# A fused attention and feed-forward kernel: which PSUM tiles are divided, one group of scores moved, the last unit's q and k turned by DMA, and the tail's attention outputs in a row

## The chip, the cores and the metric

The kernel runs on one core of one Trainium2 chip. The metric is device time in microseconds (us); a time is the median of several runs. Profiles are of one execution each.

## The reference

Inputs are q, k and v (8 batches, 12 heads, 448 rows, 64 columns, float32), w_in (768 x 2048) and w_out (2048 x 768).

```python
scores = scale * np.matmul(q, k.transpose(0, 1, 3, 2))        # scale = 1/8
m = np.max(scores, axis=-1, keepdims=True)
e = np.exp(scores - m)
attn = e / (np.sum(e, axis=-1, keepdims=True) + np.exp(-m) + 1e-09)
attn_out = np.matmul(attn, v)
x = attn_out.transpose(0, 2, 1, 3).reshape(B * S, H * D)      # 3584 x 768
h = x @ w_in
sp = np.where(h > 20.0, h, np.log1p(np.exp(np.minimum(h, 20.0))))
g = h * np.tanh(sp)                                           # Mish
out = g @ w_out                                               # 3584 x 768
```

## The kernel before

**Tiling.** Heads are taken in pairs, 48 of them, six to a batch. Each q or k of a pair is loaded as [112, 2, 256] float32 (row r of a head is 4p + t, so a partition holds four rows), cast to bf16 on GpSimd (POOL), and turned on TensorE (PE): four transposes of [112, 128] each for q and k go to a PSUM bank (`transpose_pair`), and `evac_qk` copies them to SBUF as qT and kT [128, 448], q on VectorE (DVE) with the scale 1/8, k on ScalarE (ACT). From pair 12 on POOL also copies the last 64 rows of one head and the first 64 of the other out of qT to a small tile (`q_rests`, two copies).

The scores of a pair are four steps s: three with two 128-row matmuls, one for each head, in two PSUM banks, and one (s = 3) for the 64 rows left of each head, in one bank. For each step DVE takes the negated row maxima (negm, line 289) and ACT the exponentials with their sums (line 300) into en (bf16). `denominators` and `normalise` divide by the sum; then one DMA transpose from SyncE's queue (SP) turns the whole of en to eT (line 339), after which PE makes the attention output (`av_pair`, line 372), which DVE casts to xT (line 381). eT has three buffers.

The feed-forward part of a batch is mm1 (xT by w_in, line 395, blocks f of 128 columns of the hidden layer with Mish on ACT, line 401, giving gT) and mm2 (gT by w_out, line 461, copied to o_sb by DVE and stored from SP).

**Stages.** A head loop takes pairs 0 to 5. Then `for u in range(2, 20)` goes through units of three pairs: u = 2 to 15 with attention (pairs 3u to 3u + 2), u = 16 to 19 a tail without. A unit is twelve steps n (exponentials of step n, then what is emitted behind them), followed by eight mm1 blocks f = 0 to 7 of batch (u − 2) // 2. From u = 4 on mm2 of earlier batches is cut into fills of two matmuls and put between. In units 4 to 15 the order in a step is written out in a table, GROUPED (GROUPED_LATE_AV for u = 5): ("fill", k) is k fills, ("sc", (i, ...)) are the scores of steps i of the unit, ("av0", i) and ("av1", i) the attention output of pair i of the unit before, in the first bank of score tile 0 or 1. In u = 16 the outputs of the last three pairs stand behind steps n = 0, 6 and 9 (`LAST_AV_AT`), in an mo tile each. While mm1 of a unit runs, the three pairs are normalised: the first two by DVE (behind f = 0 and f = 3), the third by POOL (behind f = 4), and the next unit's q and k are turned on PE behind f = 1, 3 and 5. Its first three score steps are ahead of f = 7.

**PSUM.** There are eight banks. Up to u = 3 three score tiles of two banks each (sc0 to sc2) and two tiles of one bank (mo) stand in one pool. At the end of u = 3 `banks_apart` gives that pool back and takes a new one: four banks of their own (b0 to b3), one tile of two banks (bb) and two of one (m0, m1). A bank on its own is released by its own reader and not by that of its neighbour. A tile of a new pool waits until the old pool's tiles that lay there have no users left.

From then on mm1's blocks use banks by MISH_BANK: 0 is the second bank of score tile 0, 1 a free mo tile, 2 the tile m1.

**Queues.** Work is in program order on each engine. SP's queue has all loads of q, k and v (issued in steps n = 0, 3, 6 for later pairs), the DMA transposes of en, and the stores. POOL has the casts of q, k and v, the copies to q_rests, the third normalise, and the DMAs that bring w_in and w_out in pieces in units 2 to 4.

Of the kernel before, what the change touches and what calls it, by code (L numbers as in the profile page):

```python
# [19 lines left out]
def kernel(  # L20
# [32 lines left out]
    def pool(name, bufs, space=None):  # L53
# [14 lines left out]
    mid_pool = pool("mid", 1)  # L68


    psum_of = tc.tile_pool(name="ps", bufs=1, space=PS)
    psum = psum_of.__enter__()
    sc_pairs = [
        psum.tile([128, 2, 512], FP32, tag=f"sc{i}", name=f"sc{i}") for i in range(3)
    ]
    sc_banks = [[t[:, j, :] for j in range(2)] for t in sc_pairs]
    mo_tiles = [psum.tile([128, 512], FP32, tag=f"mo{i}", name=f"mo{i}") for i in range(2)]
    mo_free = deque(mo_tiles)

    def banks_apart():  # L80

        flush_late()
        assert len(mo_free) == 2
        psum_of.__exit__(None, None, None)
        ps = pool("ps2", 1, PS)
        own = [ps.tile([128, 512], FP32, tag=f"b{i}", name=f"b{i}") for i in range(4)]
        last = ps.tile([128, 2, 512], FP32, tag="bb", name="bb")
        sc_pairs[:] = [None, None, last]
        sc_banks[:] = [own[0:2], own[2:4], [last[:, j, :] for j in range(2)]]
        mo_tiles[:] = [ps.tile([128, 512], FP32, tag=f"m{i}", name=f"m{i}") for i in range(2)]  # L90
        mo_free.clear()
        mo_free.append(mo_tiles[0])

    ident = singles.tile([128, 128], BF16)
    make_identity(nc, ident)
# [11 lines left out]
    for t_ in en_bufs:  # L107
# [2 lines left out]


    GROUP_FROM = 2 * HP
    q_rests = [
        singles.tile([128, 2, 64], BF16, tag=f"qr{i}", name=f"qr{i}") for i in range(UNIT_PAIRS)
    ]
# [59 lines left out]
    def cast_pair(p, with_v=True):  # L175
        if p >= N_PAIRS:
            return
        q_f, k_f = loaded[p][:2]
        q_bf = bf_pool.tile([SP_, NT, 2, D], BF16, tag="q_bf", name="q_bf")
        k_bf = bf_pool.tile([SP_, NT, 2, D], BF16, tag="k_bf", name="k_bf")  # L180
        v_bf = bf_pool.tile([SP_, 2, NT * D], BF16, tag="v_bf", name="v_bf", bufs=9)
        by_t = "p h (t d) -> p t h d"
        cast_q, cast_k = nc.gpsimd.tensor_copy, nc.gpsimd.tensor_copy
        if p == 0:
            cast_q, cast_k = nc.vector.tensor_copy, nc.scalar.copy
        cast_q(out=q_bf, in_=q_f.rearrange(by_t, t=NT))  # L186
        cast_k(out=k_bf, in_=k_f.rearrange(by_t, t=NT))  # L187
        casted[p] = (q_bf, k_bf, v_bf)
        if with_v:
            cast_v(p)  # L190

    def transpose_pair(p, bank=None):
# [16 lines left out]
        own = [] if bank is not None else [ps, ps_k] if p == 0 else [ps]  # L209
        qkT[p] = (by_s, own)  # L210

    def evac_qk(p, act=False):
        if p >= N_PAIRS:
            return
        (q_ps, k_ps), own = qkT[p]
        mo_free.extend(own)
        qT = qk_pool.tile([128, S], BF16, tag="qT", name="qT")
        kT = qk_pool.tile([128, S], BF16, tag="kT", name="kT")
        qkT[p] = (qT, kT)
        if act:  # L220
            nc.scalar.mul(qT, q_ps[:, 0:S], SCALE)
        else:
            nc.vector.tensor_scalar(
                out=qT, in0=q_ps[:, 0:S], scalar1=SCALE, scalar2=None, op0=ALU.mult
            )
        if p >= GROUP_FROM:
            q_rest = q_rests[p % UNIT_PAIRS]
            nc.gpsimd.tensor_copy(out=q_rest[0:64, 0, :], in_=qT[0:64, 384:S])
            nc.gpsimd.tensor_copy(out=q_rest[64:128, 1, :], in_=qT[64:128, 0:64])
# [252 lines left out]
    for g in range(B // 2):  # L482
# [23 lines left out]
        [("sc", (6,))],  # L506
        [],
        [("av1", 1), ("fill", 2)],
        [("sc", (7,)), ("fill", 2), ("sc", (8, 9)), ("fill", 4)],
        [("sc", (10,))],  # L510
        [],
        [("av0", 2), ("fill", 4), ("sc", (11,)), ("fill", 4)],
# [7 lines left out]
        [("sc", (6,))],  # L520
        [],
        [("av1", 0), ("fill", 2)],
        [("sc", (7,)), ("fill", 2), ("sc", (8, 9)), ("fill", 4)],
        [("sc", (10,))],
        [],
        [("av0", 1), ("sc", (11,))],
# [2 lines left out]
        [],  # L529
    )  # L530
    LATE_AV = first_mm2 + 1
    MISH_BANK = (0, 1, 2, 0, 1, 2, 1, 2)
    to_gather = deque()

    BY_POOL = 4
    LEAD = UNIT_PAIRS + 1
    LOAD_AT = (0, 3, 6)
    LAST_AV_AT = (0, 6, 9)
    HEAD = HP

    BY_PE = (2, 4, HEAD - 1, HEAD, HEAD + 1)
# [56 lines left out]
    for u in range(UNITS_PER_B, N_UNITS + 2 * UNITS_PER_B):  # L598
# [3 lines left out]
            filler.extend(mm2_part(*part))  # L602
        total, done, acc = sum(w for _, w in filler), 0, 0.0
        p0 = u * UNIT_PAIRS
        grouped = attn and p0 >= GROUP_FROM
        if u == N_UNITS:
            mo_free.append(mo_tiles[1])
# [2 lines left out]
        for n in range(steps):  # L610
# [6 lines left out]
            if grouped:  # L617
# [23 lines left out]
                        cast_pair(at + LEAD - 1)  # L641
                if u - UNITS_PER_B < len(W_AT):
                    load_w(W_AT[u - UNITS_PER_B].get(n, 0))
                continue
            if late_tp:
                evac_qk(p0 + 2)
# [26 lines left out]

        moe = u < N_UNITS + UNITS_PER_B
        b, w = (u - UNITS_PER_B) // UNITS_PER_B, u % UNITS_PER_B
        nxt = p0 + UNIT_PAIRS
# [5 lines left out]
        for f in range(FF_U):  # L682
            if f == FF_U - 1 and to_group and nxt < N_PAIRS:
                for s in range(3):
                    scores(nxt * STEPS + s)
            if moe:
                bank = sc_banks[0][0] if f == 1 else None
                if to_group:
                    bank = (sc_banks[0][1], None, mo_tiles[1])[MISH_BANK[f]]
                mm1_mish(b, w * FF_U + f, bank)  # L690
                if f == 2 and to_gather:
                    gather_mid(to_gather.popleft())
            if u == UNITS_PER_B and f in (2, 6):
                load_w(1)
            if not attn:
                continue
            if f == 0:
                denominators(att[p0]["whole"])
                normalise(todo[0], dma=todo[0] not in BY_PE)
            if f in (1, 3, 5):  # L700
                transpose_pair(nxt + f // 2, bank=f // 2 % 2)
                evac_qk(nxt + f // 2)
                if f == 1 and u > first_mm2:
                    cast_pair(nxt + UNIT_PAIRS - 1)
            if not to_group and f in (4, 6):
                scores_ahead(nxt * STEPS + f // 2 - 1)
            if f == FF_U - 1 and not to_group:
                scores_ahead(nxt * STEPS + 3)
            if f == 3:
                normalise(todo[1], dma=todo[1] not in BY_PE)  # L710
            if f == 4:
# [40 lines left out]
```

## Time and profile before

| | |
|---|---|
| median of 3 runs | 475.01 us (475.08, 474.40, 475.01) |
| profiled execution | 474.54 us |
| its span | 472.5 us |
| mean granted TensorE clock | 0.981 of full speed |
| PE busy | 437.3 us |
| ACT busy | 345.3 us |
| DVE busy | 339.0 us |
| POOL busy | 193.6 us |

The span is from the first to the last instruction in the profile; the rest of the execution's time lies around it. Busy times are sums over an engine's instructions, with overlaps counted once; they don't say which of the engines a stretch of the program waits for.

In the profiled execution unit 4 begins at 102.3 us, unit 5 at 127.5, unit 6 at 153.4; units 6 to 14 take 25.56 us each. mm1 of unit 15 begins at 399.1 us and the tail at 408.25.

Rows of a timeline have the start, the duration, engine, line, operation, output and inputs and a count; in square brackets stands the time for which the engine was idle ahead of it and what ended that. SPq and POOLq are DMA issues on those queues.

### The profile page before, as it was taken

What the parts mean: (1) busy time and instruction counts of PE and PEld (TensorE: products, weight loads), DVE (VectorE), ACT (ScalarE), POOL (GpSimd) and SP (SyncE); (2) the same over time, 40 slices, a digit from 0 to 9 for tenths busy, and PEclk for the clock granted to TensorE, in tenths of its full rate; (3) what the DMA queues carried; (4) which work ended last, traced back from release to release, by engine and by line L of the source; (5) the groups of instructions that cost most, each with busy time, mean ns of one, the idle gap of its engine ahead of it and who ended that gap; (6) DMA issues with size and microseconds to landing.
All of it is one profiled execution on the core that took longest, in us unless ns stands there. A gap on an engine that the chain in (4) does not pass through costs nothing.

```text
span 472.5 us, 8903 instructions
## 1 busy us (share of the span) xinstructions
PE 437.3 (93%) x3048; PEld 235.9 (50%) x3048; DVE 339.0 (72%) x723; ACT 345.3 (73%) x919; POOL 193.6 (41%) x365
## 2 busy tenths in 40 slices
PE   4565887799999999999999999999999999999997
PEld 2233444454544464555555554646454555555565
DVE  4788987958777897879787888788787978320021
ACT  5979787769797888979797979798897979312300
POOL 4876808364515354443636163525444360300000
PEclk9998698899999999999999999999999999999999
DMA  8999959999999979899989989998989794960213
GB/s 222 225 238 214 246 86 238 181 168 203 207 230 265 209 199 204 246 197 266 181 210 219 239 165 248 217 224 226 201 237 216 216 185 103 168 147 1 68 33 102
DMA packets 202382, 90.37 MB, mean 191 GB/s; under 512 B 159073, under 2 KB 198881, under 8 KB 202337
## 3 DMA queue, kind: packets, MB, share of 16 engines
q1 hardware_dynamic: 194848, 83.51, 80.9%
q0 software_dynamic: 7488, 6.29, 8.8%
q8 instruction: 24, 0.39, 0.3%
q14 instruction: 22, 0.17, 0.1%
HBM read 45.61 MB, written 11.01 MB: 120 GB/s over the span
## 4 chain that ended last, share of the span: by engine, by line
PE 75%; DVE 2%; DMA 1%; ACT 1%; issue 1%; POOL 0%; SPq 0%; DVEq 0%; POOLq 0%
PE m L461 32%; PE m L395 21%; PE b L372 6%; PE b L395 6%; PE b L263 4%; PE bb L263 2%; PE b L204 1%; PE bb L204 1%; PE m L271 1%; DMA q_f<-in_q_dram 1%; DVE negm L289 1%; PE m L372 1%; DVE o_sb L448 1%; ACT en L300 0%; POOL q_bf L186 0%
## 5 line engine op out<-in xcount | busy, mean ns | idle before, releaser
L461 PE MATMUL m<-w_out_sb,gT 128*128 128x384 bf16 (+1 forms) x896 | 141.8, 304 | 0.7 <-DVE o_sb L448 0.7
L395 PE MATMUL m<-xT,w_in_sb 128*128 128x448 bf16 x552 | 115.4, 352 | 0.0
L461 PEld LDWEIGHTS <-gT 128*128 128x128 bf16 x896 | 80.6, 98 | 59.1 <-issue 20.7
L395 PEld LDWEIGHTS <-w_in_sb 128*128 128x128 bf16 x768 | 71.6, 98 | 67.5 <-issue 9.7
L401 ACT ACTIVATE gT<-m 128x448 bf16<-128x448 f32 x92 | 50.2, 547 | 68.7 <-PE m L395 68.7
L333 POOL TENSOR_SCALAR en<-en,rden 128x448 bf16<-128x448 bf16 x122 | 76.4, 645 | 52.9 <-DVE rden L325 41.2
L289 DVE TENSOR_REDUCE negm<-b 128x1 f32<-128x448 f32 x144 | 79.9, 617 | 24.3 <-PE b L266 24.3
L300 ACT ACTIVATE en<-b,negm 128x448 bf16<-128x448 f32 x144 | 89.6, 646 | 0.0
L186 POOL CAST q_bf<-q_f 112x512 bf16<-112x512 f32 x47 | 28.9, 615 | 111.9 <-DMA q_f<-in_q_dram 111.2
L448 DVE COPY o_sb<-m 128x384 f32<-128x384 f32 (+1 forms) x64 | 32.2, 503 | 48.1 <-PE m L461 44.3
L335 DVE TENSOR_SCALAR en<-en,rden 128x448 bf16<-128x448 bf16 x214 | 66.0, 377 | 0.5
L300 ACT ACTIVATE en<-sc,negm 128x448 bf16<-128x448 f32 x84 | 52.8, 647 | 8.6 <-DVE negm L289 4.6
L289 DVE TENSOR_REDUCE negm<-sc 128x2 f32<-128x896 f32 (+1 forms) x48 | 45.5, 968 | 10.9 <-PE sc L266 4.0
L300 ACT ACTIVATE en<-bb,negm 128x448 bf16<-128x448 f32 x72 | 45.2, 638 | 5.8 <-DVE negm L289 5.8
L289 DVE TENSOR_REDUCE negm<-bb 128x2 f32<-128x896 f32 x36 | 39.0, 1082 | 0.0
L395 PE MATMUL b<-xT,w_in_sb 128*128 128x448 bf16 x168 | 36.5, 352 | 2.5 <-ACT en L300 1.8
L372 PE MATMUL b<-eT,v_bf 112*64 112x448 bf16 x288 | 34.1, 357 | 0.0
L173 POOL CAST v_bf<-v_f 112x512 bf16<-112x512 f32 x48 | 29.9, 622 | 6.5 <-DMA v_f<-in_v_dram 6.2
L187 POOL CAST k_bf<-k_f 112x512 bf16<-112x512 f32 x47 | 29.2, 621 | 6.3 <-DMA k_f<-in_k_dram 5.7
L300 ACT ACTIVATION_READ_ACCUMULATOR en<-b,negm 128x1 f32 x144 | 31.5, 219 | 0.0
L372 PEld LDWEIGHTS <-v_bf 112*64 112x64 bf16 x384 | 19.5, 111 | 19.2 <-issue 12.6
L263 PE MATMUL sc<-kT,qT 64*128 64x448 bf16 x36 | 16.7, 479 | 12.6 <-ACT en L300 11.2
(75 smaller groups left out, 573.1 us busy)
## 6 DMA issues: line engine op xcount, KB each, us to landing
q_f<-in_q_dram SPq DMA_DIRECT2D x48, 224.0 KB, 4.7
k_f<-in_k_dram SPq DMA_DIRECT2D x48, 224.0 KB, 4.9
v_f<-in_v_dram SPq DMA_DIRECT2D x48, 224.0 KB, 5.2
w_in_sb<-in_moe_w_in_dram POOLq DMA_DIRECT2D x12, 256.0 KB, 6.2
w_out_sb<-in_moe_w_out_dram POOLq DMA_DIRECT2D x8, 384.0 KB, 6.6
out_dram<-o_sb SPq DMA_DIRECT2D x7, 336.0 KB, 3.3
out_dram<-o_sb SPq DMA_DIRECT2D x8, 288.0 KB, 4.0
out_dram<-o_sb SPq DMA_DIRECT2D x8, 240.0 KB, 4.1
```

The source lines that it names most:

```text
L173: nc.gpsimd.tensor_copy(out=casted[p][2], in_=loaded.pop(p)[2])
L187: cast_k(out=k_bf, in_=k_f.rearrange(by_t, t=NT))
L263: nc.tensor.matmul(sc[0][:, 0:S], lhsT=qT[0:64, qa : qa + 128], rhs=kA, start=True, stop=True)
L289: nc.vector.tensor_reduce(out=negm, in_=scored, axis=AX.X, op=ALU.max, negate=True)
L300: nc.scalar.activation(out=st["en"][:, :, c, 0:SP_], in_=sc[bk][:, 0:S].rearrange("q (j c) -> q j c", j=NT), func=AF.Exp, bias=st["negm"][ ...
L333: nc.gpsimd.tensor_scalar(scalar2=1.0, op0=ALU.mult, op1=ALU.mult, **args)
L335: nc.vector.tensor_scalar(scalar2=None, op0=ALU.mult, **args)
L372: nc.tensor.matmul(av[h * 64 : (h + 1) * 64, 0:S], lhsT=v_bf[:, h, j * D : (j + 1) * D], rhs=e_h, start=(j == 0), stop=(j == NT - 1),)
L395: nc.tensor.matmul(h_ps[:, 0:S], lhsT=w_in_sb[:, dm, ff * 128 : (ff + 1) * 128], rhs=xT[b][:, dm, :], start=(dm == 0), stop=(dm == DM_T - 1),)
L401: nc.scalar.activation(out=gT[b][:, ff, :], in_=h_ps[:, 0:S], func=AF.Mish)
L448: nc.vector.tensor_copy(out=o_sb[:, cols], in_=st["o"][:, 0:n_cols])
L461: nc.tensor.matmul(st["o"][:, 0:n_cols], lhsT=src[:, ff, c0 : c0 + 128], rhs=w_out_sb[:, ff, cols], start=(ff == 0), stop=(ff == FF_T - 1),)
```

## The change

Five edits:

- **PSUM.** sc2 and the two mo tiles now stay in a pool of their own for the whole program; only sc0 and sc1 are in a pool that `banks_apart` gives back, for four banks of their own. As in the kernel before, one mo tile is taken out of the free list there. The first mm1 after it takes its banks in another order, FIRST_MISH_BANK, which begins with the mo tiles.
- **Mish banks.** The fourth mm1 block of a unit writes the first bank of score tile 0 (new number 3) instead of the bank of the first block.
- **Score order.** In both tables the scores of steps 8 and 9 come behind one fill instead of two; the fill goes behind them.
- **Turns by DMA.** q and k of pairs 45 and 46 (two of the last unit's three) are not turned on PE. POOL casts q with the scale in it, and two DMA transposes for each pair on SP, behind steps 8 and 11 of u = 14, write qT and kT. Their copies to q_rests go behind f = 3.
- **Tail.** In u = 16 the three attention outputs come one after the other behind n = 9, in the first bank of score tile 0, 1 and 2. The last pair's normalise in u = 15 is on DVE instead of POOL.

```diff
-    psum_of = tc.tile_pool(name="ps", bufs=1, space=PS)
-    psum = psum_of.__enter__()
-    sc_pairs = [
-        psum.tile([128, 2, 512], FP32, tag=f"sc{i}", name=f"sc{i}") for i in range(3)
-    ]
-    sc_banks = [[t[:, j, :] for j in range(2)] for t in sc_pairs]
+    psum = pool("ps", 1, PS)
+    last_pair = psum.tile([128, 2, 512], FP32, tag="sc2", name="sc2")
     mo_tiles = [psum.tile([128, 512], FP32, tag=f"mo{i}", name=f"mo{i}") for i in range(2)]
     mo_free = deque(mo_tiles)
+    pairs_of = tc.tile_pool(name="ps_pairs", bufs=1, space=PS)
+    psum = pairs_of.__enter__()
+    sc_pairs = [
+        psum.tile([128, 2, 512], FP32, tag=f"sc{i}", name=f"sc{i}") for i in range(2)
+    ] + [last_pair]
+    sc_banks = [[t[:, j, :] for j in range(2)] for t in sc_pairs]
 
     def banks_apart():
         flush_late()
+        mo_tiles[:] = mo_free
         assert len(mo_free) == 2
-        psum_of.__exit__(None, None, None)
-        ps = pool("ps2", 1, PS)
+        mo_free.pop()
+        pairs_of.__exit__(None, None, None)
+        ps = pool("ps_banks", 1, PS)
         own = [ps.tile([128, 512], FP32, tag=f"b{i}", name=f"b{i}") for i in range(4)]
-        last = ps.tile([128, 2, 512], FP32, tag="bb", name="bb")
-        sc_pairs[:] = [None, None, last]
-        sc_banks[:] = [own[0:2], own[2:4], [last[:, j, :] for j in range(2)]]
-        mo_tiles[:] = [ps.tile([128, 512], FP32, tag=f"m{i}", name=f"m{i}") for i in range(2)]
-        mo_free.clear()
-        mo_free.append(mo_tiles[0])
+        sc_pairs[0:2] = [None, None]
+        sc_banks[0:2] = [own[0:2], own[2:4]]
...
+    TURN_BY_DMA = (N_PAIRS - UNIT_PAIRS, N_PAIRS - UNIT_PAIRS + 1)
...
-        cast_q(out=q_bf, in_=q_f.rearrange(by_t, t=NT))
+        if p not in TURN_BY_DMA:
+            cast_q(out=q_bf, in_=q_f.rearrange(by_t, t=NT))
+        else:
+            nc.gpsimd.tensor_scalar(
+                out=q_bf, in0=q_f.rearrange(by_t, t=NT),
+                scalar1=SCALE, scalar2=1.0, op0=ALU.mult, op1=ALU.mult,
+            )
...
+    def turn_by_dma(p):
+        pair = [qk_pool.tile([128, S], BF16, tag=t, name=t) for t in ("qT", "kT")]
+        for dst, src in zip(pair, casted[p]):
+            nc.sync.dma_start_transpose(
+                out=dst.rearrange("c (t q) -> c t q", q=SP_),
+                in_=src.rearrange("q t h d -> q (t h d)"),
+            )
+        qkT[p] = pair
+
+    def rest_of(p):
+        qT, q_rest = qkT[p][0], q_rests[p % UNIT_PAIRS]
+        nc.gpsimd.tensor_copy(out=q_rest[0:64, 0, :], in_=qT[0:64, 384:S])
+        nc.gpsimd.tensor_copy(out=q_rest[64:128, 1, :], in_=qT[64:128, 0:64])
...
-        [("sc", (7,)), ("fill", 2), ("sc", (8, 9)), ("fill", 4)],
+        [("sc", (7,)), ("fill", 1), ("sc", (8, 9)), ("fill", 5)],
...
-    MISH_BANK = (0, 1, 2, 0, 1, 2, 1, 2)
+    MISH_BANK = (0, 1, 2, 3, 1, 2, 1, 2)
+    FIRST_MISH_BANK = (1, 2, 0, 1, 2, 0, 1, 2)
...
-    LAST_AV_AT = (0, 6, 9)
+    TURN_AFTER = (8, 11)
+    LAST_AV_AT = 9
...
+                if n in TURN_AFTER and nxt + TURN_AFTER.index(n) in TURN_BY_DMA:
+                    turn_by_dma(nxt + TURN_AFTER.index(n))
...
-            elif u == N_UNITS and n in LAST_AV_AT:
-                av_pair(p0 - UNIT_PAIRS + LAST_AV_AT.index(n))
+            elif u == N_UNITS and n == LAST_AV_AT:
+                for i in range(UNIT_PAIRS):
+                    av_pair(p0 - UNIT_PAIRS + i, bank=sc_banks[i][0])
...
-                    bank = (sc_banks[0][1], None, mo_tiles[1])[MISH_BANK[f]]
+                    order = FIRST_MISH_BANK if nxt == GROUP_FROM else MISH_BANK
+                    bank = (sc_banks[0][1], None, mo_tiles[1], sc_banks[0][0])[order[f]]
...
-                transpose_pair(nxt + f // 2, bank=f // 2 % 2)
-                evac_qk(nxt + f // 2)
+                if nxt + f // 2 not in TURN_BY_DMA:
+                    transpose_pair(nxt + f // 2, bank=f // 2 % 2)
+                    evac_qk(nxt + f // 2)
...
                 normalise(todo[1], dma=todo[1] not in BY_PE)
+                for p in TURN_BY_DMA:
+                    if p // UNIT_PAIRS == u + 1:
+                        rest_of(p)
...
-                normalise(todo[2], dma=todo[2] not in BY_PE, on_pool=True)
+                normalise(todo[2], dma=todo[2] not in BY_PE, on_pool=u + 1 < N_UNITS)
```

More of the change, by code (lines that the diff above doesn't have):

```diff
@@ L226, in evac_qk @@
         if p >= GROUP_FROM:
-            q_rest = q_rests[p % UNIT_PAIRS]
-            nc.gpsimd.tensor_copy(out=q_rest[0:64, 0, :], in_=qT[0:64, 384:S])
-            nc.gpsimd.tensor_copy(out=q_rest[64:128, 1, :], in_=qT[64:128, 0:64])
+            rest_of(p)
         if p == 0 or own and not act:
@@ L522 @@
         [("av1", 0), ("fill", 2)],
-        [("sc", (7,)), ("fill", 2), ("sc", (8, 9)), ("fill", 4)],
+        [("sc", (7,)), ("fill", 1), ("sc", (8, 9)), ("fill", 5)],
         [("sc", (10,))],
@@ L604 @@
         p0 = u * UNIT_PAIRS
+        nxt = p0 + UNIT_PAIRS
         grouped = attn and p0 >= GROUP_FROM
@@ L675 @@
         b, w = (u - UNITS_PER_B) // UNITS_PER_B, u % UNITS_PER_B
-        nxt = p0 + UNIT_PAIRS
         todo = sorted(range(p0, nxt), key=lambda p: p in BY_PE)
@@ L710 @@
                 normalise(todo[1], dma=todo[1] not in BY_PE)
+                for p in TURN_BY_DMA:
+                    if p // UNIT_PAIRS == u + 1:
+                        rest_of(p)
             if f == 4:
-                normalise(todo[2], dma=todo[2] not in BY_PE, on_pool=True)
+                normalise(todo[2], dma=todo[2] not in BY_PE, on_pool=u + 1 < N_UNITS)
         if attn and u + 1 < N_UNITS:
```

## The prediction

> **What bounds the kernel now.** I read the page first: the busy times by engine, then the chain that ended last.
>
> ```profile
> PE 437.3 (93%) x3048; PEld 235.9 (50%) x3048; DVE 339.0 (72%) x723; ACT 345.3 (73%) x919; POOL 193.6 (41%) x365
> PE 75%; DVE 2%; DMA 1%; ACT 1%; issue 1%; POOL 0%; SPq 0%; DVEq 0%; POOLq 0%
> ```
>
> TensorE (PE) carries the end. An average over stages does not say where it can be shortened, so I next read the stretches of the units. One in the steady part:
>
> ```profile
> 204.59:230.15 25.56, 25.56 (x182) 13.57 (x183) 20.92 (x47) 21.53 (x57) 11.13 (x23) 1.00 1.05 216
> ```
>
> The columns are the stretch, its length, then the busy us (and instructions) of PE, weight loads, DVE, ACT and POOL, the granted clock and two DMA columns. PE is busy for all 25.56 us. In such a unit (u=6 to u=14) an edit is worth something only if it takes instructions off PE or removes a stall between them, and there is none left. So the gains must come from the places where PE stalls: the start of u=4 (the new PSUM banks), u=4 and u=5, and the tail. I looked for them in PE's timeline, where a bracket is idle time and its releaser.
>
> **A: two score tiles divided, not all PSUM tiles renewed.** The last products of u=3 and the first matmul block (mm1) after the bank change, from the timeline of all engines:
>
> ```profile
> 88.79 1.71 PE L372 MATMUL mo<-eT,v_bf 112*64 112x448 bf16 x16
> ...
> 90.48 1.15 DVE L381 CAST xT<-mo 128x448 bf16<-128x448 f32 x2
> ...
> 91.52 0.65 ACT L300 ACTIVATE en<-sc,negm 128x448 bf16<-128x448 f32 x1
> ...
> 92.31 0.92 PE L395 MATMUL b<-xT,w_in_sb 128*128 128x448 bf16 x4 [1.81 <-ACT en L300]
> ```
>
> Before, all eight banks are given back and taken anew, so the block waits for the last exponential of the old pool (91.52 + 0.65 = 92.17). After, the first block writes an mo tile, which stays, and waits only for that tile's cast: the first of two casts, 90.48 + 1.15/2 = 91.06. The gain on PE is 92.31 − 91.2 = 1.1 us. The second block takes the other mo tile (cast over at 91.63) and starts 1.14 us after the first, and the third takes a divided bank at about 93.4, past 92.17: no new wait.
>
> **B and C.** Stalls of u=4, from PE's timeline, and one steady unit's third group of scores, from the timelines of DVE and PE:
>
> ```profile
> 117.89 0.35 PE L395 MATMUL b<-xT,w_in_sb 128*128 128x448 bf16 x1 [0.29 <-DVE xT L381]
> ...
> 121.32 1.30 PE L395 MATMUL b<-xT,w_in_sb 128*128 128x448 bf16 x6 [0.41 <-ACT gT L401]
> ```
>
> ```profile
> 214.55 0.61 DVE L381 CAST xT<-b 128x448 bf16<-128x448 f32 x1
> ...
> 214.79 0.81 PE L461 MATMUL m<-w_out_sb,gT 128*128 128x384 bf16 x4
> 215.54 0.36 PE L263 MATMUL b<-kT,qT 64*128 64x448 bf16 x1
> ...
> 215.74 0.35 PE L263 MATMUL b<-kT,qT 64*128 64x448 bf16 x1
> ...
> 215.93 2.22 DVE L289 TENSOR_REDUCE negm<-b 128x1 f32<-128x448 f32 x4 [0.24 <-PE b L266]
> ```
>
> B gives the fourth Mish block a bank of its own instead of the first block's, which takes away the 0.41 us at 121.32. C moves the products sc(8, 9) ahead of one fill of two matmuls, half of the row of four: (215.54 − 214.79)/2 = 0.37 us. The DVE waits 0.24 us for these scores now and the scores would come 0.37 us sooner, so DVE and ACT run up to 0.24 us earlier in each grouped unit. PE issues the same work in another order, so in steady units it gains nothing. The second pair's bank is free when the cast at 214.55 ends (215.16); its new start, 215.74 − 0.37 = 215.37, clears that by 0.2 us. If that cover went, each of twelve units would lose what the cast is late, at most 0.37 us. In u=4 the earlier DVE takes up to 0.24 of the 0.29 us at 117.89. A, B and C together bring PE 1.1 + 0.4 + 0.25 = 1.75 us forward at the end of u=4.
>
> **What of that survives u=5.** There the transposes of the next keys wait for POOL's casts, which wait for loads on SP's queue. SP rows, the POOL rows and the DMA queues between 121.9 and 124.4 us (packets, mean us, share of the stretch), then POOL and PE in u=5:
>
> ```profile
> 95.25 4.28 SPq L339 DMA_TRANSPOSE eT<-en  x1
> ...
> 99.83 4.33 SPq L339 DMA_TRANSPOSE eT<-en  x1
> ...
> 121.86 14.86 SPq L339 DMA_TRANSPOSE eT<-en  x3
> ```
>
> ```profile
> 100.04 4.34 POOL L333 TENSOR_SCALAR en<-en,rden 128x448 bf16<-128x448 bf16 x7 [1.40 <-DVE rden L325]
> ...
> 117.89 1.48 POOL L169 DMA_DIRECT2D w_out_sb<-in_moe_w_out_dram  x2
> ...
> 147.53 0.62 POOL L187 CAST k_bf<-k_f 112x512 bf16<-112x512 f32 x1
> ```
>
> ```profile
> q0 software_dynamic: 659, 0.49, 130.5%
> ```
>
> ```profile
> 148.20 0.37 PE L204 MATMUL b<-ident,k_bf 112*128 112x112 bf16 x4 [0.26 <-POOL k_bf L187]
> ...
> 151.26 0.37 PE L204 MATMUL b<-ident,k_bf 112*128 112x112 bf16 x4 [0.22 <-POOL k_bf L187]
> ```
>
> PE reaches these two transposes 0.26 and 0.22 us too early already; whatever it arrives sooner is waited away unless the casts move. The casts hang on u=5's loads, and these stand on SP behind the three transposes issued from 121.86, which take 14.86 instead of about 13 us. In their first 2.5 us the only queue that moves data is POOL's (q0, the w_out pieces issued up to 119.37). Those pieces stand on POOL behind casts of earlier loads, behind u=3's transposes on SP. What A can close there is SP's idle time between u=3's transposes: 99.83 − 99.53 = 0.30, and from 99.83 + 4.33 = 104.16 to the end of POOL's normalise (104.38) 0.22 us, together 0.5. The first transpose's own input hangs on the exponentials of u=3 and does not move. So the chain moves by 0.45 to 0.5 us; if u=4's transposes, issued some 1.7 us sooner, also begin moving sooner, by up to 1.75. The least is 0.25 (only one gap closes). I take 0.7, near the end that rows carry.
>
> The Trainium skill ("DMA: Bandwidth & Descriptors", section "Queues, rings and completion order") says that each DMA engine takes turns between the queues for which it has work, packet by packet. By that the transposes would have begun at 121.86 beside the w_out pieces, and would begin sooner when issued sooner; the trace does not agree so far, since the one row of that stretch is q0's. By the rule the sum would be that of the first rival.
>
> **D: q and k of pairs 45 and 46 turned by DMA.** PE and SP in u=14 and at the start of u=15, and the tile eT between 375 and 400 us (issue ns least, median, most; then us to landing):
>
> ```profile
> 381.18 0.36 PE L204 MATMUL bb<-ident,q_bf 112*128 112x112 bf16 x4
> ...
> 381.57 1.30 PE L395 MATMUL m<-xT,w_in_sb 128*128 128x448 bf16 x6
> ...
> 387.55 0.95 PE L372 MATMUL b<-eT,v_bf 112*64 112x448 bf16 x8
> ```
>
> ```profile
> 371.26 0.46 SPq L143 DMA_DIRECT2D v_f<-in_v_dram  x1
> 377.94 13.34 SPq L339 DMA_TRANSPOSE eT<-en  x3
> ```
>
> ```profile
> 374.21 0.62 POOL L187 CAST k_bf<-k_f 112x512 bf16<-112x512 f32 x1 [0.18 <-DMA k_f<-in_k_dram]
> ```
>
> ```profile
> L339 SPq DMA_TRANSPOSE eT<-en x3: 4207/4327/4591, 377.9 to 387.0; - x3
> DMA to landing us min/median/max: 6.1/7.1/7.8
> ```
>
> Eight transposes of a pair take PE from 381.18 to 381.57, 0.39 us. Two pairs: 0.8 us off PE in a stage where PE never idles. Two evacuations on DVE and two on ACT go with them, which bring nothing there. What is added: four DMA transposes on SP and two scaled casts on POOL. SP is idle from 371.72 to 377.94. An attention transpose has 28 blocks of 128 columns and issues in 4.33 us, one of q or k has 4, so by blocks 0.62 us each and 2.5 us in all; the upper bound is 4.33 us each. Pair 46's key cast ends at 374.83, so its two turns would end by about 376.1, before 377.94. I take the block price because a load issues in 0.46 us (371.26): no more than that can be fixed, and with 0.46 fixed and 4/28 of the rest a turn costs 1.0, still over by 377. The scaled cast takes POOL about a seventh of a normalise (4.34/7 = 0.62), as long as the plain cast, off the path. D is worth 0.8, from 0.4 (the first scores of u=15 wait for the landing) to 0.8.
>
> **E: three attention outputs in a row in the tail, the last normalise on DVE.** PE's and SP's timelines there:
>
> ```profile
> 408.25 3.41 PE L461 MATMUL m<-w_out_sb,gT 128*128 128x384 bf16 x20
> 411.73 0.95 PE L372 MATMUL m<-eT,v_bf 112*64 112x448 bf16 x8
> 412.61 4.08 PE L461 MATMUL m<-w_out_sb,gT 128*128 128x384 bf16 x24
> 416.62 0.95 PE L372 MATMUL m<-eT,v_bf 112*64 112x448 bf16 x8
> 417.50 1.61 PE L461 MATMUL m<-w_out_sb,gT 128*128 128x384 bf16 x12
> 419.04 0.95 PE L372 MATMUL m<-eT,v_bf 112*64 112x448 bf16 x8
> 419.92 0.83 PE L461 MATMUL m<-w_out_sb,gT 128*128 128x192 bf16 x8
> 420.70 1.29 PE L395 MATMUL m<-xT,w_in_sb 128*128 128x448 bf16 x6
> ```
>
> ```profile
> 403.14 13.55 SPq L339 DMA_TRANSPOSE eT<-en  x3
> ```
>
> Start to start, 24 matmuls take 416.62 − 412.61 = 4.01, or 0.167 each. By that the 20 would take 3.34 and took 3.48; the twelve (four of 384 columns, eight of 192) 1.34 and took 1.54; the last eight of 192, 0.67 and took 0.78. The surplus, 0.14 + 0.20 + 0.11 = 0.45 us, I read as waits for an mo tile, which the outputs take and DVE must empty. After, they write score banks, so this goes. An output alone takes 0.88 from its start to the next one's; the two in a row at 88.79 last 1.71, so the second adds 0.76: twice 0.12 saved. Sum 0.7. The third output then starts near 418.4 and needs the third turned block: SP issues it at about 403.14 + 2 × 4.5 = 412.2, landing 6.1 us or more later, 418.3 or more. It is a tie, so down to 0.3 remains. The DVE normalise, costed at nothing, ends before SP reaches it either way, since the three transposes issue without a gap (13.55 against three times 4.33).
>
> **Sum.** 474.54 − 0.7 − 0.8 − 0.7 = 472.3 for the profiled execution; its span is 472.5 and 2.0 lie around it. The median of the runs is 0.5 above the profiled execution, so 472.8.
>
> **Rivals.** First: all of A to C reaches the end, because u=4's transposes start sooner with their issue. Then 1.75 + 0.8 + 0.7 = 3.25, and 471.8 (471.1 if C and E bring a few tenths more). For it: SP issues them when en is normalised, which moves. Against: q0 alone in 121.9 to 124.4.
> Second: the change does little of what it says, because the hidden chains give the same due times: u=5's casts move by 0.25 only, the third output waits for its landing (0.3), and the first scores of u=15 wait for the turned q and k (D 0.3). That is 0.85, and 474.2. For it: two ties that I could not decide; against: each needs its own miss.
> Third, slower: the turns block SP. If the issue time is by instruction and not by block, four turns take 17.3 us from 371.72; the first attention transpose is issued at 389.0 instead of 377.94 and av(42), due at 387.55, has its block at 389.0 + 6.1 = 395.1 or later, 7.6 us late or more. Less the 2.2 of the rest this is 5.4 us slower, 480.4. It decides from about 2.2 us a turn: a block that lands 7.1 us after its issue must be issued by 387.55 − 7.1 = 380.45 for av(42), and (380.45 − 371.72)/4 = 2.2. For it: no row shows a transpose this small. Against: one of 28 blocks takes only 4.3.
>
> **How the numbers follow.** The forecast has 0.64, the first rival 0.14, the second 0.11, the third 0.11. The forecast's own range is 472.3 to 473.6 (terms 0.45 + 0.6 + 0.4 to 1.1 + 0.8 + 0.8). The range for 8 in 10 reaches down into the first rival, 471.3, and up to the second, 474.2. About 0.2%, 0.95 us, is what a measurement of this kernel can tell from no change: below 474.06 is faster, so forecast and first rival, 0.78; the second rival is the same, 0.11; the third slower, 0.11.
>
> **What would show it.** A: the idle time before the first mm1 of u=4 falls from 1.81 to about 0.7 with DVE as releaser. B: no bracket on Mish in u=4. What survives: the brackets on k_bf in u=5 grow to some 0.7 each or in sum to over 1; if they stay small, the first rival holds. D: u=14's mm1 stage is 0.8 shorter, four turns of about 0.6 us on SP, and en(42)'s transpose issued before 378; a turn over 2.2 us would make the third rival. E: the stretch from the first tail fill to the first tail mm1 falls from 12.45 to 11.7, and its bracket says whether the third output waits for DMA. The unit period stays at 25.56; if it changes, the reading of C is wrong.

## The result and the profile after

The changed kernel takes 471.25 us (median of 4 runs, 470.86 to 472.3) against 474.97 of the kernel before in the same set: ratio 0.9928, 95% interval 0.9909 to 0.9947. In two later sets, each beside the kernel before on the same chip, it came to 0.9954 (0.9938 to 0.9971) and 0.9949 (0.9932 to 0.9967). It is faster, by 2.2 to 3.7 us. The profiled execution takes 471.56 us with a span of 469.7: 3.0 and 2.8 less than before.

The page after, busy times and the chain that ended last:

```profile
PE 435.9 (93%) x3032; PEld 234.8 (50%) x3032; DVE 336.6 (72%) x727; ACT 344.2 (73%) x917; POOL 188.4 (40%) x358
PE 79%; DVE 7%; ACT 7%; DMA 3%; issue 2%; POOL 2%; SPq 0%; DVEq 0%; ACTq 0%; POOLq 0%
```

PE still carries the end and has 16 instructions fewer, the turns of two pairs. That tells little of where 2.8 us went, so I cut both executions at the same matmuls of PE's timeline (starts of the rows named; each column is a length in us):

| kernel | start of u=3's last scores | from there to u=4's first qr scores | to u=6's first | one unit of u=6 to u=14 | u=14's third qr scores to u=15's first | first tail fill to first tail mm1 |
|---|---|---|---|---|---|---|
| before | 88.49 | 15.84 | 51.16 | 25.57 | 12.87 | 12.45 |
| changed | 88.53 | 14.66 | 51.78 | 25.50 | 12.09 | 11.62 |
| difference | 0.04 | −1.18 | +0.62 | −0.07 | −0.78 | −0.83 |

The unit is a mean of eight; before, most units take 25.56 us and two take 25.59 and 25.61. Ten units (u=6 to u=15) at 0.06 make 0.6. The sum is −1.18 + 0.62 − 0.6 − 0.78 − 0.83 = −2.8, the difference of the spans; the stretches that the table leaves out differ by about 0.1 us.

**A, B, C in u=3 to u=5.** PE, with its brackets:

```profile
91.17 2.43 PE L414 MATMUL mo<-xT,w_in_sb 128*128 128x448 bf16 x12 [0.64 <-DVE xT L400]
...
120.92 0.36 PE L211 MATMUL sc<-ident,q_bf 112*128 112x112 bf16 x4 [0.35 <-DVE qT L244]
...
146.62 0.37 PE L211 MATMUL sc<-ident,q_bf 112*128 112x112 bf16 x4 [0.51 <-POOL q_bf L188]
147.17 0.37 PE L211 MATMUL b<-ident,k_bf 112*128 112x112 bf16 x4 [0.19 <-POOL k_bf L194]
...
150.18 0.37 PE L211 MATMUL sc<-ident,q_bf 112*128 112x112 bf16 x4 [0.36 <-POOL q_bf L188]
150.73 0.37 PE L211 MATMUL b<-ident,k_bf 112*128 112x112 bf16 x4 [0.19 <-POOL k_bf L194]
```

The idle time ahead of the first mm1 fell from 1.81 to 0.64, and the stalls at 117.89 and 121.32 are gone. A new one of 0.35 stands at 120.92: q of the second pair is turned into the second half of a two-bank tile whose first half DVE has yet to copy out. Then the casts of u=5 take most back: their brackets grew from 0.48 to 1.25 in sum. SP shows why:

```profile
95.27 12.97 SPq L358 DMA_TRANSPOSE eT<-en  x3
108.29 0.57 SPq L144 DMA_DIRECT2D q_f<-in_q_dram  x1
...
120.63 15.63 SPq L358 DMA_TRANSPOSE eT<-en  x3
136.31 0.57 SPq L144 DMA_DIRECT2D q_f<-in_q_dram  x1
```

u=4's transposes are issued 1.23 us sooner than before (121.86) and end 0.46 sooner (136.26 against 136.72). One stall of u=5 stands in every profile of this study, before and after, at 0.71 or 0.72 us, and no edit touches it: a fill, at 130.69 in the changed kernel, waits for DVE's copy of o_sb.

**C in the steady units.** One unit before and after, PE and DVE around the third attention output, first of the kernel before:

```profile
217.72 0.95 PE L372 MATMUL b<-eT,v_bf 112*64 112x448 bf16 x8
218.67 0.82 PE L461 MATMUL m<-w_out_sb,gT 128*128 128x192 bf16 x8
```

```profile
218.07 0.55 DVE L448 COPY o_sb<-m 128x384 f32<-128x384 f32 x1
```

and of the changed kernel:

```profile
217.04 0.95 PE L391 MATMUL b<-eT,v_bf 112*64 112x448 bf16 x8
217.92 0.83 PE L480 MATMUL mo<-w_out_sb,gT 128*128 128x192 bf16 x8
218.59 0.35 PE L290 MATMUL mo<-kT,qr 128*128 128x448 bf16 x1
```

```profile
217.07 0.55 DVE L467 COPY o_sb<-mo 128x384 f32<-128x384 f32 x1
```

Before, the fill starts 0.95 us behind the output, 0.05 after DVE's copy of o_sb ends (218.07 + 0.55 = 218.62): it waits for the one mo tile. After, the copy ends at 217.62 and the fill follows in 0.88. No bracket shows this wait of 0.07: the ends of matmuls are modelled and pipelined, and the row's 0.95 covers it. DVE's rows of the four negm have no gap in front of them any more.

**D and E.** SP in u=14, the tile eT between 375 and 400 us, and the tail on PE and SP:

```profile
371.12 1.18 SPq L222 DMA_TRANSPOSE qT<-q_bf  x1
372.42 1.84 SPq L222 DMA_TRANSPOSE kT<-k_bf  x1
374.37 1.20 SPq L222 DMA_TRANSPOSE qT<-q_bf  x1
375.73 1.19 SPq L222 DMA_TRANSPOSE kT<-k_bf  x1
377.02 13.27 SPq L358 DMA_TRANSPOSE eT<-en  x3
...
400.89 13.45 SPq L358 DMA_TRANSPOSE eT<-en  x3
```

```profile
L358 SPq DMA_TRANSPOSE eT<-en x3: 4205/4337/4527, 377.0 to 385.9; - x3
DMA to landing us min/median/max: 6.1/7.1/7.8
```

```profile
406.24 8.62 PE L480 MATMUL mo<-w_out_sb,gT 128*128 128x384 bf16 x56
414.80 1.70 PE L391 MATMUL b<-eT,v_bf 112*64 112x448 bf16 x16
416.33 0.92 PE L391 MATMUL sc<-eT,v_bf 112*64 112x448 bf16 x8
417.19 0.83 PE L480 MATMUL mo<-w_out_sb,gT 128*128 128x192 bf16 x8
417.86 1.30 PE L414 MATMUL mo<-xT,w_in_sb 128*128 128x448 bf16 x6
```

The turns took 1.2 to 1.8 us and were over before 377.02. The three outputs run without a bracket; the third eT landed at 415.82, 0.5 us before its output starts.

The same code does not reach u=3's last scores at the same time: over the profiles of this study that start lies between 88.1 and 92.6 us. From u=6 on the mean unit repeats to 0.04 us and the stages of D and E to 0.05, where the text names no cause. So the experiments are read by stages; medians carry the head's spread.

### The profile page after: what moved, and what is told of

It reads as the page before. It is cut to its first block, busy times and chain, and to the rows that moved or that the text cites. A ratio compares the mean times of both kernels' runs of the same rounds, so it can differ in the third digit from the quotient of the medians.

```text
span 469.7 us, 8871 instructions
## 1 busy us (share of the span) xinstructions
PE 435.9 (93%) x3032; PEld 234.8 (50%) x3032; DVE 336.6 (72%) x727; ACT 344.2 (73%) x917; POOL 188.4 (40%) x358
## 4 chain that ended last, share of the span: by engine, by line
PE 79%; DVE 7%; ACT 7%; DMA 3%; issue 2%; POOL 2%; SPq 0%; DVEq 0%; ACTq 0%; POOLq 0%
PE mo L480 30%; PE mo L414 23%; PE b L391 6%; PE b L414 6%; ACT en L319 5%; DVE negm L308 5%; PE b L282 3%; PE sc L282 3%; PE sc L211 2%; PE mo L369 2%; PE b L211 1%; PE mo L290 1%; DMA q_f<-in_q_dram 1%; DMA w_in_sb<-in_moe_w_in_dram 1%; DMA k_f<-in_k_dram 1%
## 5 line engine op out<-in xcount | busy, mean ns | idle before, releaser
L480 PE MATMUL mo<-w_out_sb,gT 128*128 128x384 bf16 (+1 forms) x896 | 141.5, 304 | 0.7 <-DVE o_sb L467 0.7
L414 PE MATMUL mo<-xT,w_in_sb 128*128 128x448 bf16 x594 | 124.3, 352 | 1.2 <-DVE xT L400 0.6
L420 ACT ACTIVATE gT<-mo 128x448 bf16<-128x448 f32 x99 | 53.7, 544 | 71.8 <-PE mo L414 71.5
L319 ACT ACTIVATE en<-sc,negm 128x448 bf16<-128x448 f32 x156 | 97.8, 641 | 11.5 <-DVE negm L308 8.2
L308 DVE TENSOR_REDUCE negm<-sc 128x2 f32<-128x896 f32 x84 | 84.3, 1015 | 11.2 <-PE sc L285 4.0
L352 POOL TENSOR_SCALAR en<-en,rden 128x448 bf16<-128x448 bf16 x115 | 71.8, 642 | 36.0 <-DVE rden L344 28.6
L467 DVE COPY o_sb<-mo 128x384 f32<-128x384 f32 (+1 forms) x64 | 32.2, 503 | 49.1 <-PE mo L480 45.3
L282 PE MATMUL sc<-kT,qT 64*128 64x448 bf16 x72 | 29.5, 418 | 12.7 <-ACT en L319 11.2
L391 PE MATMUL b<-eT,v_bf 112*64 112x448 bf16 x304 | 35.8, 357 | 0.0
L319 ACT ACTIVATION_READ_ACCUMULATOR en<-sc,negm 128x1 f32 x156 | 33.0, 212 | 0.0
L285 PE MATMUL sc<-kT,qT 64*128 64x448 bf16 x72 | 29.8, 422 | 0.0
```

Source lines behind the costliest of these rows:

```text
L282: nc.tensor.matmul(sc[0][:, 0:S], lhsT=qT[0:64, qa : qa + 128], rhs=kA, start=True, stop=True)
L285: nc.tensor.matmul(sc[1][:, 0:S], lhsT=qT[64:128, qb : qb + 128], rhs=kB, start=True, stop=True)
L308: nc.vector.tensor_reduce(out=negm, in_=scored, axis=AX.X, op=ALU.max, negate=True)
L319: nc.scalar.activation(out=st["en"][:, :, c, 0:SP_], in_=sc[bk][:, 0:S].rearrange("q (j c) -> q j c", j=NT), func=AF.Exp, bias=st["negm"][ ...
L352: nc.gpsimd.tensor_scalar(scalar2=1.0, op0=ALU.mult, op1=ALU.mult, **args)
L391: nc.tensor.matmul(av[h * 64 : (h + 1) * 64, 0:S], lhsT=v_bf[:, h, j * D : (j + 1) * D], rhs=e_h, start=(j == 0), stop=(j == NT - 1),)
```

## The experiments

**C alone** and **all but C**:

```diff
-        [("sc", (7,)), ("fill", 2), ("sc", (8, 9)), ("fill", 4)],
+        [("sc", (7,)), ("fill", 1), ("sc", (8, 9)), ("fill", 5)],
```

(in both tables, on the kernel before)

> The kernel before with C alone (the scores of steps 8 and 9 one fill sooner in both tables). Theory 1, a stall that the busy time of PE hides: in each grouped unit the first fill behind the third attention output waits 0.07 us for the copy of the o_sb tile on DVE, which C brings forward by 0.24 us. Then a steady unit takes 25.50 instead of 25.56 us, the start of u=6 moves by no more than 0.1, and the end is 0.6 us earlier (10 units by 0.06): span 471.9, 0.6 off the median of the kernel before. Theory 2, C is worth nothing on PE, and the shorter units come from the PSUM tiles that A leaves in place: units stay at 25.56, span 472.5.

Span 471.8; 474.48 us, ratio 0.998 (0.9961 to 1.0). A unit takes 25.50 us, the stages of D and E stay at 12.88 and 12.44. C alone also takes away the 0.29 us of u=4 on the cast xT; the 0.41 us that B is for stays:

```profile
121.77 1.29 PE L395 MATMUL b<-xT,w_in_sb 128*128 128x448 bf16 x6 [0.41 <-ACT gT L401]
```

From u=3's last scores to u=6's first qr scores this run took 66.27 us, 0.73 less than the kernel before and no more than the changed kernel's 66.44, with no bracket on a cast in u=5, though A and B are not in it. And the other way round, the same lines put back in the changed kernel:

> The changed kernel with C undone (steps 8 and 9 behind two fills as before). Theory 1 (hidden stall): units go back to 25.56 us, u=6 still starts 0.5 us earlier than in the kernel before, and the end is 0.6 us later than in the changed kernel: span 470.3. Theory 2 (A's tiles make the units shorter): units stay at 25.50, span 469.7. In both, the matmul of u=4's first mm1 block that waits for the cast xT waits 0.3 us again, which u=5 takes up.

A unit takes 25.56 again, and the other stages stay as changed (12.09, 11.67). In u=4 the 0.29 us are back and B's stall stays away:

```profile
117.20 0.35 PE L414 MATMUL b<-xT,w_in_sb 128*128 128x448 bf16 x1 [0.29 <-DVE xT L400]
```

Together they settle it: the 0.06 us a unit are C's, by the wait for the o_sb copy, and A's tiles have no part in it. From the third output's start to the fill's it is 0.94 or 0.95 us in each of ten units of every profile without C (here, before, and one below), and 0.88 in each of ten of every profile with it. The span was 471.4, 1.7 and not 0.6 above the changed kernel's: the head was 0.4 later, and u=3's last scores to u=6 took 67.09 instead of 66.44, where POOL issued the pieces of w_out at 115.63 instead of 114.30. I don't count that as C's: other profiles of the changed kernel have 66.3 to 67.5 there.

**The pieces of w_out earlier in u=4:**

```diff
-    W_AT = (..., {3: 1, 5: 1, 7: 1, 9: 1})
+    W_AT = (..., {0: 2, 1: 2})
```

> The changed kernel with the last four pieces of w_out issued from POOL behind steps 0 and 1 of u=4 (two each) instead of behind steps 3, 5, 7 and 9: at about 105.5 to 108.5 us, before the casts that wait for u=4's loads. Theory 1, the loads of u=5 hold back what A, B and C win, and stand behind transposes that wait for the w_out pieces on the DMA engines: the three transposes of u=4 issue in about 13 us instead of 15.6, u=5's loads come 2.6 us sooner, the brackets on q_bf and k_bf in u=5 (0.51, 0.19, 0.36, 0.19) go, and the start of u=6 and the end are 1.0 us earlier: span 468.7. Theory 2, the pieces take the DMA engines from something that is as urgent (loads of u=4, its casts behind the issues on POOL): u=4 then shows a new wait on casts and the end is the same or later, span 469.7 to 471.

Span 468.8; 470.87 us, ratio 0.992 (0.9904 to 0.9936). u=4's first qr scores to u=6's take 50.75 us, 1.03 less than in the changed kernel, with no bracket on casts in u=5: theory 1's number. But theory 2 has a part too: u=4 has two new stalls, 0.44 on eT and 0.45 on a cast.

**The pieces one by one:**

```diff
+    W_AT = (..., {0: 1, 1: 1, 3: 1, 5: 1})
```

> The changed kernel with the last four pieces of w_out behind steps 0, 1, 3 and 5 of u=4, one each. With two each behind 0 and 1 the stalls of u=5 were gone, but u=4 had two new ones (0.44 on eT, 0.45 on a cast), since all four pieces took the DMA engines from the loads and transposes there. Theory 1 (the loads of u=5 hold the gain back, and stand behind transposes that wait for the pieces): two pieces fewer behind 117 us let u=4's transposes begin by about 122, the loads of u=5 come some 1.5 us sooner than in the changed kernel, so the start of u=6 and the end are up to 1.2 us earlier (span 468.4), with at most 0.4 of new stalls in u=4. Theory 2 (the DMA engines are full whatever the order): u=5's stalls come back in part and the span is 469.2 to 469.7.

Neither: span 471.5, 473.57 us, ratio 0.998 (0.9966 to 0.9994), and 53.52 us from u=4 to u=6, 1.7 more. u=5's stalls on casts are gone, but DVE's first normalise of u=4 took 3.60 us, and PE waited 1.90 behind it. After that wait TensorE's granted clock fell to 0.51. DVE and POOL in that run, and two stretches behind the wait (columns as in the prediction):

```profile
118.54 3.60 DVE L354 TENSOR_SCALAR en<-en,rden 128x448 bf16<-128x448 bf16 x7
```

```profile
119.30 1.48 POOL L170 DMA_DIRECT2D w_out_sb<-in_moe_w_out_dram  x2
120.77 0.63 POOL L188 CAST q_bf<-q_f 112x512 bf16<-112x512 f32 x1
121.34 0.68 POOL L194 CAST k_bf<-k_f 112x512 bf16<-112x512 f32 x1
```

```profile
123.80:127.30 3.50, 3.50 (x18) 1.92 (x16) 1.53 (x8) 1.09 (x2) 2.04 (x5) 0.51 1.29 229
127.30:130.00 2.70, 2.70 (x18) 1.12 (x17) 1.37 (x4) 1.08 (x2) 2.64 (x6) 1.00 1.27 227
```

In the changed kernel POOL is idle from 118.99 to 120.92 and the same seven instructions take 2.06 us. From the turn that waited to u=5's first scores PE took 5.96 us here and 4.28 there, so the lower clock cost about as much as the wait. This run doesn't tell how the pieces' places alone compare.

**The pieces in u=2:**

```diff
-    W_AT = ({5: 1, 9: 1}, {...}, {3: 1, 5: 1, 7: 1, 9: 1})
+    W_AT = ({5: 1, 9: 1, 10: 2, 11: 2}, {...}, {})
```

> The changed kernel with four more pieces of w issued behind steps 10 and 11 of u=2 (at about 60 us, where the DMA engines are 26 to 69% busy and POOL is idle) and none in u=4; the order of the pieces is the same, so w_out's last four come in u=3. The runs before moved them within u=4, and either new waits on DMA came there (two each behind steps 0 and 1), or POOL's casts ran into DVE's normalise, which took 3.60 instead of 2.06 us (one each behind 0, 1, 3, 5). Theory 1 (u=5's loads hold back what A, B and C win, since they stand behind transposes that wait for the pieces): u=4's three transposes issue in about 13 us, the stalls on q_bf and k_bf in u=5 go, no new wait comes in u=4, and from the start of u=4 to that of u=6 it takes 50.5 us (51.78 in the changed kernel): 1.2 us earlier at the end. Theory 2 (those stalls have another cause): the stretch stays above 51.5 us.

Span 468.3; 470.34 us, ratio 0.9898 (0.9882 to 0.9914): the lowest median of the study, beside 472.67 of the changed kernel in the same set. u=4 to u=6 takes 50.22. SP, and the two brackets that are left at the turns of u=4 and u=5, both on DVE's copies of qT:

```profile
120.62 12.96 SPq L358 DMA_TRANSPOSE eT<-en  x3
133.63 0.57 SPq L144 DMA_DIRECT2D q_f<-in_q_dram  x1
```

```profile
120.90 0.36 PE L211 MATMUL sc<-ident,q_bf 112*128 112x112 bf16 x4 [0.27 <-DVE qT L244]
...
146.39 0.36 PE L211 MATMUL sc<-ident,q_bf 112*128 112x112 bf16 x4 [0.30 <-DVE qT L244]
```

The transposes were issued at the same time as in the changed kernel and take 12.96 us instead of 15.63. The one queue that moved data from 123.6 to 124.2 us in the changed kernel is POOL's, and from 121.8 to 122.4 in this run it is the other (packets, MB, share of the stretch; the middle figure of the prediction's queue row is MB too, not us):

```profile
q0 software_dynamic: 145, 0.11, 127.0%
```

```profile
q1 hardware_dynamic: 470, 0.12, 102.7%
```

So what A, B and C win in u=4 was held in u=5 by these loads, and the loads by the pieces.

**The same move in the kernel before**, for what is left to A, B and C:

> The kernel before with the pieces of w moved as in w_mid (two each behind steps 10 and 11 of u=2, none in u=4). From the last score matmul of u=3 to the third-from-last kind of landmark, the first qr matmul of u=6, it took 67.0 us in the kernel before, 66.3 to 67.1 in four profiles of the changed kernel and its tail variants, and 64.9 in w_mid. Theory 1 (A, B and C are worth their 1.75 us only where u=5's loads are early): moving the pieces alone takes away the stalls of u=5 that the kernel before has (0.26 and 0.22 by the brackets, 0.8 from start to start), so 66.2 to 66.5, and the rest to 64.9 is A, B and C. Theory 2 (the pieces alone bring it): 65.0, and A, B and C bring nothing there. By the end, span 471.5 in the first, 470.3 in the second.

Theory 1: u=3's last scores to u=6 take 66.38 us (67.00 before, 64.90 in the run above), so by these profiles the pieces alone bring 0.6 and A, B and C 1.5 more once u=5 lets them through. The 0.6 is not told from the spread, since C alone came to 66.27 with the pieces where they were; the 1.5 is more than the 1.2 us by which profiles of the changed kernel differ there, but it rests on one profile of each kernel. On the median nothing is seen (474.58 us, 1.0002, 0.9979 to 1.0026), and its span of 471.8 is 0.7 below the page of before.

**Turns twice:** each of the four turns once more, into tiles that nothing reads.

```diff
+        for i, src in enumerate(casted[p][:2]):
+            nc.sync.dma_start_transpose(
+                out=spare[i].rearrange("c (t q) -> c t q", q=SP_),
+                in_=src.rearrange("q t h d -> q (t h d)"),
+            )
```

> The changed kernel with each of the four turns of q and k issued a second time, into spare tiles that nothing reads. It measures how much room SP has there. The four turns took 1.2 to 1.8 us each; four more take 5 us. Theory 1, the first attention transpose of u=14 is then issued about 5 us later (382 instead of 377.0), lands at 388.5 to 390 and the first attention output of u=15, at 385.63, waits 3 to 4 us; the end is 3 to 4 us later, span 473. Theory 2, a turn is held for its own input and not by SP, the four more fit into the gaps between, and the end is no more than 0.5 us later.

Span 475.0; 477.25 us, ratio 1.0045 (1.0032 to 1.0058): slower than the kernel before. The first attention transpose was issued at 383.32 us. PE's wait, and the stretches around it (length, busy times of the engines, then the granted clock, 1.00 in the first row):

```profile
389.57 1.06 PE L398 MATMUL b<-eT,v_bf 112*64 112x448 bf16 x8 [3.23 <-DMA eT<-en]
```

```profile
384.00:389.50 5.50, 2.35 (x15) 1.17 (x12) 2.27 (x4) 5.47 (x16) 1.91 (x5) 1.00 1.02 190
389.50:392.60 3.10, 3.02 (x14) 1.10 (x15) 0.62 (x1) 0.47 (x2) 0.00 (x0) 0.63 1.16 216
392.60:395.30 2.70, 2.70 (x17) 1.06 (x16) 2.11 (x4) 1.45 (x5) 0.00 (x0) 0.80 1.78 203
```

Theory 1 by its mechanism (a wait of 3.2), but u=15 became 4.8 us longer: after the wait the granted clock was 0.63 and then 0.80, and the other 1.6 us go with that (from this output's start to the next one's PE took 6.01 us, 4.47 in the changed kernel). So the wait that the third rival names is real, and four turns at 1.35 us in the mean stay clear of it by little: eT of the first pair lands at about 384.1 and its output starts at 385.63. In the other profiles with four turns this margin is 0.7 to 1.2 us; in the kernel before it was 2.5.

**The tail's outputs apart**, in mo tiles as before and in score tiles:

```diff
-            elif u == N_UNITS and n == LAST_AV_AT:
-                for i in range(UNIT_PAIRS):
-                    av_pair(p0 - UNIT_PAIRS + i, bank=sc_banks[i][0])
+            elif u == N_UNITS and n in LAST_AV_AT:          # (0, 6, 9)
+                i = LAST_AV_AT.index(n)
+                av_pair(p0 - UNIT_PAIRS + i)                # second run: bank=sc_banks[i][0]
```

> The changed kernel with the tail's three attention outputs back behind steps 0, 6 and 9, in mo tiles, and the last normalise still on DVE. Theory 1, E's 0.83 us come from the outputs' place alone (no wait for an mo tile, 0.45; two outputs in a row, 0.24; a little more): the stretch from the first tail fill to the first tail mm1 takes 12.4 us again instead of 11.62, span 470.5. Theory 2, part of it came from the normalise on DVE, by an earlier third eT: then less than 0.8 comes back and the outputs wait less than in the kernel before.

> As the run before, but the three outputs behind steps 0, 6 and 9 write the first banks of the score tiles, as in the changed kernel. It parts the two halves of E. If the waits for mo tiles are worth 0.45 and the row 0.24, the tail stretch takes 11.62 + 0.24 to 0.4 = 11.9 to 12.0 us; if the row is what counts, 12.4; if the tiles are all of it, 11.6.

The tail stretch took 12.45 us and 12.07 (471.1 and 472.6 by span, with heads at 88.34 and 90.47; ratios 0.9977, 0.9956 to 0.9999, and 0.996, 0.9941 to 0.998). So leaving the mo tiles is worth 0.38 and the row 0.45. Of the row's 0.45, the outputs themselves are 0.25 (2.39 us for the three, from 414.80 to 417.19, against three times 0.88); the other 0.20 is in the fills: the 48 matmuls of 384 columns take 7.80 us in one piece and 8.00 in the three pieces of the second run (3.34, 4.00 and 0.66).

**The last normalise on POOL again:**

```diff
-                normalise(todo[2], dma=todo[2] not in BY_PE, on_pool=u + 1 < N_UNITS)
+                normalise(todo[2], dma=todo[2] not in BY_PE, on_pool=True)
```

> The changed kernel with the last normalise of u=15 on POOL again. It is costed at nothing: SP issues the three last transposes without a gap (13.45 us in the changed kernel), and POOL is done before the third's turn. Then the tail's stretch from first fill to first mm1 stays at 11.62 us. If the normalise on DVE mattered, the third transpose is issued later than 8.9 us after the first, and the third output in the row waits for its landing.

The tail stretch is 11.62 us, to the digit, and the third transpose was issued 8.7 us after the first. The span of 475.0 (477.19 us, one run) is the head's: u=3's last scores started at 92.63.

**The changed kernel again**, twice:

> The changed kernel itself once more, to be timed beside the other runs of this call and to see how far its profile repeats: the unit period (25.50), the 0.8 of D and the 0.8 of E should be the same to 0.02 us, while the start of u=4 and the stalls of u=5 may move by half a microsecond with the DMA traffic of the head.

> The changed kernel once more, to be timed beside the run before on one chip: 0.9928 and 0.9954 of the kernel before so far. From the start of u=4 to that of u=6 51.6 to 51.9 us, unit period 25.50.

472.62 and 472.67 us; spans 471.3 and 470.7. Units of 25.50, the stages of D and E 12.08 and 11.61 or 11.62 in both; u=4's first qr scores to u=6's 51.88 and 51.62; heads at 89.99 and 89.62.

## Why the prediction was right, and where it was not

The sign was right, and the size on the profile near: 2.2 forecast, 2.8 to 3.0 measured. The first median alone (471.25) lies at the lower end of the range and nearer to the first rival's 471.8 than to the forecast's 472.8 (the later ones, 472.62 and 472.67, are near the forecast). But that rival is refuted by the sign that the prediction gave for it: the brackets on the casts of u=5 did not stay small. Those on k_bf are 0.19 each, but new ones of 0.51 and 0.36 on q_bf stand ahead of them, 1.25 in sum, and in the other profiles of the changed kernel with the pieces in u=4 as before the sum is 1.2 to 2.2. By term:

- **A and B at u=4**: forecast 1.1 and 0.4. By u=4's first qr scores 1.18 was won; by the last turn of u=4, 1.54 (125.12 to 123.58 us, the starts of u=4's last turn), of which the new 0.35 on DVE had been taken. B's 0.41 and C's 0.29 are shown apart by the first two experiments. Not foreseen: the new stall, which the 0.41 had covered.
- **What survives u=5**: forecast 0.45 to 0.5 by the rows, taken as 0.7. The profile has 0.56 from u=3's last scores to u=6's first qr scores (67.00 to 66.44), by the steps that were named: SP's loads 0.46 sooner, pieces of w_out 0.38 sooner, transposes that begin no sooner for being issued sooner. Six later profiles of the changed kernel's front have 66.3 to 67.5 there, and C alone has 66.27. So this term is not shown: 0.7 was too much, and what A and B bring past u=5 with the pieces in u=4 is not told from nothing.
- **The first rival's rule.** The Trainium skill ("DMA: Bandwidth & Descriptors", section "Queues, rings and completion order") has each DMA engine take turns between queues by packets. These runs don't show that for transposes: in the run with the pieces in u=2 data move from about 1.2 us after the same issue at 120.6; in the changed kernel POOL's queue is alone until past 124. Whether the transposes' packets stood in their queue by then, and were passed over, no run tells.
- **C**: this step failed. It was costed at nothing in the steady units because PE has no bracket there and is busy for 25.56 of 25.56 us. It was worth 0.06 us in each of ten, 0.6 in all, nearly the whole miss of the profile's sum. "The unit period stays at 25.56" was the sentence that the profile refuted; it named the right test. That the later medians come so near to the forecast is in part luck: C's 0.6, D and E make 2.2 us without the surviving term, which was taken as 0.7.
- **D**: forecast 0.8, measured 0.78. The price of a turn was wrong by two (0.62 forecast, 1.2 to 1.8 measured; the fixed part is more than the 0.46 taken as the most), without harm, since a margin was left between the landing of eT and its output, 1.5 us in this profile. Room on SP was not the reason: the last turn ends at 376.92 and the attention transpose follows at 377.02.
- **E**: forecast 0.7, measured 0.83. The tiles 0.45 forecast and 0.38 measured, the row 0.24 and 0.45: the outputs themselves saved the 0.24, and the 0.20 that fills save by running in one piece was overlooked. The tie with the third landing went well, by 0.5 us.

The first set's median fell 0.9 us more than the spans of the two profiles; the later sets, 2.2 and 2.6 us. I take that for the head's spread, which no term here touches; it is not shown, since only one execution of each run is profiled.

## What to carry to other kernels

A busy share of 100% on a pipelined engine doesn't exclude a stall: set the start of an instruction against the end of what it needs on the other engine, and compare the distance of starts with the same pair elsewhere. A gain upstream is worth what the next external due time lets through; find that due time's own chain (here loads behind transposes behind weight pieces) and move its first link to where the queue is idle. When the start of a program scatters more than the effect, compare stages between fixed instructions, and in more than one profile of each kernel.

## What the runs showed of the hardware

- After a wait of 3.23 us PE's granted clock was 0.63 over the next 3.1 us and 0.80 over the 2.7 after. The Trainium skill ("TensorE: Matmul & The Clock Gate", "Part 1: The HAM clock gate") puts the fall at about 3.4 us of idleness, to half the clock. The depth agrees: 0.51 over 3.5 us in the run with the pieces one by one. The time doesn't: in that run the fall followed a wait of 1.90 us, while the wait of 1.81 us ahead of u=4 in the kernel before was followed by none.
- DVE's seven normalise instructions took 3.60 us while POOL issued DMAs and cast, 2.06 with POOL mostly idle. The Trainium skill ("SBUF — State Buffer", section "Who interferes with whom") says that the two share a pair of ports and one waits for the other's whole instruction in DVE's fast modes. The rows agree with such a wait; they don't show which instruction waited for which.
- A DMA transpose of 4 blocks holds SP's queue 1.2 us in most cases (1.84 once in four), one of 28 blocks 4.3. If both have the same fixed part and a price by block, about 0.7 us is fixed, (28 × 1.2 − 4 × 4.3)/24: an estimate from two sizes.
- An issue of transposes while POOL's queue keeps the DMA engines busy holds SP longer: the first of u=4's took 6.22 us in the changed kernel and 4.13 with the pieces in u=2.
